# V without a shifted copy, five tiles for transposed probabilities, and PV of unit i-4 ordered behind the scores of unit i

## The chip, the cores and the metric

The kernel runs on one core of a Trainium2 chip. TensorE multiplies matrices, VectorE (DVE), ScalarE (ACT) and GpSimd (POOL) work on elements, and SyncE (SP) issues most transfers from a queue of its own; 16 DMA engines carry them. The engines run beside each other and wait for each other through semaphores; each takes its own instructions strictly in order. The metric is the device time of the whole program in microseconds.

## The reference, cut to what matters

```python
q_rot, k_rot = (rotate(q), rotate(k))          # (4, 8, 576, 64), rotary
scores = scale * np.matmul(q_rot, k_rot.transpose(0, 1, 3, 2))
attn = np.exp(scores - scores.max(-1)) / (sum + 1e-09)
x = np.matmul(attn, v)                         # to (2304, 512)
h = np.maximum(np.maximum(x @ w1, x @ w2), x @ w3)
x = h @ w_out                                  # (2304, 512)
# then each token goes to the expert with the largest logit of x @ w_gate:
out[mask] = gate * (np.maximum(xe @ w1[e], 0.0) @ w2[e])
```

All inputs are float32. The kernel multiplies in float16 pairs: a number is split into a high and a low half, and a product is the sum of high by high, high by low and low by high.

## The kernel before

The program has three parts: attention over 4 batches, a dense layer (the three products, their maximum, `w_out`) whose work is mixed into attention, and the routed layer, which starts after attention at about 606 us.

Attention is cut into 36 units a batch, 144 in all: four query blocks of 128 by eight heads, and four units for the 64 queries that are left. One unit goes through this chain:

- S(i): TensorE multiplies one query block with all 576 keys into a score bank (lines 636, 637 in batch 0, 643 to 646 and 656 later). There are two banks.
- VectorE scales the scores and takes the minimum (659); ScalarE takes the exponential into `p32` and its float16 high half (661, 663).
- VectorE makes the low half (668), 576 columns. `p16` then holds 576 high and 576 low columns side by side.
- SP issues one DMA that transposes the 1152 columns in nine blocks of 128 into a tile `pt` (671). There are three `pt` tiles.
- PV(i): TensorE multiplies the blocks with V in 14 matmuls (695, 696, 698, 699).

576 is four and a half blocks of 128. So the fifth block holds the last 64 high columns and the first 64 low columns, and all later low blocks lie 64 positions off. The kernel therefore keeps a second copy of V's high half, shifted by 64 positions across the partitions, in the same tile (`v2`); two DMAs for each half batch write it (606, 607), and two ScalarE instructions fill its ends (608, 609).

Each batch needs preparation: `prep_qk` loads, rotates, splits and transposes queries and keys of four heads at a time (three transposing DMAs of 18 blocks, lines 485, 486, 490), `prep_v` loads and splits V. Three buffers for transposed keys rotate, so the second half of a batch can only be transposed once the first half of the batch before is through.

A scheduler places the instructions of each engine in a fixed order: each has a priority (`self.at(...)`, in units of attention) and is placed once it believes its inputs to be ready. PV is called `LAG` = 3 units behind S, but its place on TensorE is the scheduler's. Dense-layer matmuls (799 to 801, 847 to 849) carry later priorities and fill in between; here they are called other work.

Of the kernel before, what the change touches and what calls it, by code (L numbers as in the profile page):

```python
# [10 lines left out]
F16 = mybir.dt.float16  # L11
BF16 = mybir.dt.bfloat16
# [10 lines left out]
P = 128  # L23
# [47 lines left out]
class K:  # L71
# [490 lines left out]
    def prep_v(self, b):  # L562
# [4 lines left out]
        def load():  # L567
            if b == 0:
                both = self.att.tile([P, 6, DM], F32, tag="kq0", name="vraw0", bufs=1).rearrange("p f c -> p (f c)")
            for hf in range(2):  # L570
                st["v", hf] = vp.tile([P, 56, D], F16, tag=f"v{hf}", name=f"v{hf}", bufs=1)
# [11 lines left out]
        def stats():  # L583
            sums = self.small.tile([P, 2], F32, name="v_sums")
            for hf in range(2):
                st["v2", hf] = st["v", hf][:, 32:52].rearrange("p (h r) d -> p h r d", h=4)
                nc.scalar.activation(st["v2", hf].rearrange("p a b d -> p (a b d)").bitcast(BF16),
                                     st[hf].rearrange("p a b -> p (a b)"), AF.Square, accum_out=sums[:, hf:hf + 1])
# [8 lines left out]
        def conv(hf):  # L597
            def go():
                s, x = st["s"], st[hf]
                vt, v2 = st["v", hf], st["v2", hf]  # L600
# [4 lines left out]
                vh4 = vh.rearrange("p (h r) d -> p h r d", r=4)  # L605
# [6 lines left out]
                self.V[b, hf] = (vh4, vl.rearrange("p (h r) d -> p h r d", r=4), v2, vt[:, 52:56])  # L612
                self.V[b, "inv"] = st["inv"]
            return go
# [3 lines left out]
    def attention(self, b):  # L618
# [5 lines left out]
        def s_part(i):  # L624
# [5 lines left out]
            if b == 0:  # L630
# [6 lines left out]
                nc.tensor.matmul(ps[:, 1, :64], lhsT=q, rhs=kt[pr, j, 512:S], start=True, stop=True)  # L637
# [605 lines left out]
LAG = 3  # L1243
# [43 lines left out]
```

## Time and profile before

| | us |
|---|---|
| median of 3 runs | 932.07 |
| lowest and highest | 930.55, 932.56 |
| profiled execution | 929.0 |
| its span | 927.2 |
| TensorE busy | 782.3 |
| VectorE busy | 670.2 |
| ScalarE busy | 574.5 |
| GpSimd busy | 249.5 |

The span is the time from the first to the last instruction. TensorE's busy time is modelled and too long, since matmuls overlap; the spacing of their starts in the timeline tells more. A wait is the idle time of an engine before an instruction, put down to what ended it. The granted clock of TensorE is a share of 2.4 GHz; it takes two levels, 1.2 and 2.4 GHz.

### The profile page before, as it was taken

What the parts mean: (1) busy time and instruction counts of PE and PEld (TensorE: products, weight loads), DVE (VectorE), ACT (ScalarE), POOL (GpSimd) and SP (SyncE); (2) the same over time, 40 slices, a digit from 0 to 9 for tenths busy, and PEclk for the clock granted to TensorE, in tenths of its full rate; (3) what the DMA queues carried; (4) which work ended last, traced back from release to release, by engine and by line L of the source; (5) the groups of instructions that cost most, each with busy time, mean ns of one, the idle gap of its engine ahead of it and who ended that gap; (6) DMA issues with size and microseconds to landing.
All of it is one profiled execution on the core that took longest, in us unless ns stands there. A gap on an engine that the chain in (4) does not pass through costs nothing.

```text
span 927.2 us, 18852 instructions
## 1 busy us (share of the span) xinstructions
PE 782.3 (84%) x7304; PEld 641.5 (69%) x7304; DVE 670.2 (72%) x1338; ACT 574.5 (62%) x1001; POOL 249.5 (27%) x245
## 2 busy tenths in 40 slices
PE   2568899889766887879898898995899999998995
PEld 1345677677644666668677677785798889997994
DVE  6988988967796776687765687542848787765771
ACT  3677877745674765565763576521834797774772
POOL 8330003234231042131112100003312744423320
PEclk9995558999987999899989999998899999998999
DMA  8699777994999988979985799713210211133110
GB/s 250 154 218 220 194 141 118 202 176 104 157 165 136 164 140 152 143 129 150 125 132 85 106 144 128 123 39 121 107 31 30 69 47 46 44 117 137 43 36 20
DMA packets 270646, 112.24 MB, mean 121 GB/s; under 512 B 246319, under 2 KB 262847, under 8 KB 270032
## 3 DMA queue, kind: packets, MB, share of 16 engines
q1 hardware_dynamic: 260992, 81.40, 52.5%
q0 software_dynamic: 9552, 29.51, 9.9%
q8 instruction: 61, 1.00, 0.5%
q14 instruction: 41, 0.34, 0.1%
HBM read 74.97 MB, written 9.80 MB: 91 GB/s over the span
## 4 chain that ended last, share of the span: by engine, by line
PE 36%; DMA 15%; issue 4%; DVE 4%; ACT 2%; POOL 2%; SPq 0%; POOLq 0%; ACTq 0%; DVEq 0%
DMA pt<-p 7%; DMA out<-o,di 5%; PE mm L800 4%; PE mm L799 4%; PE mm L801 4%; PE pa L1201 3%; PE pa L1200 3%; PE pa L1202 3%; PE pb L1172 3%; PE pb L1170 3%; PE pb L1171 3%; PE mm L847 1%; PE mm L849 1%; DMA kq<-kls 1%; PE mm L848 1%
## 5 line engine op out<-in xcount | busy, mean ns | idle before, releaser
L799 PE MATMUL mm<-xT,w 128*128 128x256 f16 (+1 forms) x792 | 195.7, 262 | 3.1 <-DVE hm L815 2.6
L800 PE MATMUL mm<-xT,w 128*128 128x256 f16 (+1 forms) x792 | 195.7, 262 | 0.0
L801 PE MATMUL mm<-xT,w 128*128 128x256 f16 (+1 forms) x792 | 195.0, 261 | 0.0
L661 ACT ACTIVATE p<-s,bi 128x576 f32<-128x576 f32 x144 | 105.6, 734 | 82.1 <-DVE s L659 58.7
L668 DVE SCALAR_TENSOR_TENSOR p<-p,p 128x576 f16<-128x576 f32 x144 | 121.5, 846 | 26.8 <-ACT p L663 26.5
L695 PE MATMUL o<-v,pt 128*128 128x64 f16 (+1 forms) x576 | 63.0, 208 | 68.9 <-DMA pt<-p 64.8
L659 DVE TENSOR_SCALAR_CACHE_REDUCE s<-s,qk_sc 128x576 f32<-128x576 f32 x108 | 87.7, 820 | 35.2 <-PE s L646 27.7
L695 PEld LDWEIGHTS <-pt 128*128 128x128 f16 x576 | 47.7, 106 | 84.0 <-DMA pt<-p 76.7
L1109 ACT CAST h<-r 128x512 fp32r<-128x512 f32 x80 | 93.7, 1209 | 18.2 <-DMA r<-moe_w,widx 13.7
L663 ACT ACTIVATE p<-p 128x576 f16<-128x576 f32 x144 | 96.7, 679 | 6.0 <-DMA pt<-p 4.0
L1110 DVE TENSOR_TENSOR l<-r,h 128x512 fp32r<-128x512 f32 x80 | 90.1, 1165 | 5.1 <-ACT h L1109 4.6
L799 PEld LDWEIGHTS <-w 128*128 128x128 f16 x792 | 80.9, 102 | 13.3 <-DVE hm L815 2.0
L800 PEld LDWEIGHTS <-w 128*128 128x128 f16 x792 | 80.2, 101 | 11.1 <-issue 2.7
L801 PEld LDWEIGHTS <-w 128*128 128x128 f16 x792 | 80.7, 102 | 8.8 <-issue 0.7
L1200 PE MATMUL pa<-xh,h 128*128 128x256 f32 x288 | 81.5, 286 | 0.8 <-ACT xh L1131 0.8
L1201 PE MATMUL pa<-xl,h 128*128 128x256 f32 x288 | 81.6, 284 | 0.2 <-DVE xl L1132 0.2
L1202 PE MATMUL pa<-xh,l 128*128 128x256 f32 x288 | 81.6, 284 | 0.0
L847 PE MATMUL mm<-oh,h 128*128 128x256 f16 (+1 forms) x216 | 61.8, 288 | 4.8 <-DVE hm L815 3.4
L1172 PE MATMUL pb<-h,hl 128*128 128x512 f32 x152 | 61.6, 408 | 3.1 <-DVE hl L1204 3.0
L696 PE MATMUL o<-v,pt 128*128 128x64 f16 (+1 forms) x576 | 62.7, 207 | 1.1 <-DVE v L604 1.1
L1170 PE MATMUL pb<-h,hh 128*128 128x512 f32 x152 | 61.6, 408 | 0.9 <-ACT hh L1203 0.9
L927 POOL DMA_INDIRECT islot<-rows,pi x18 | 19.2, 1069 | 159.1 <-DVE pi L917 93.3
(303 smaller groups left out, 2092.4 us busy)
## 6 DMA issues: line engine op xcount, KB each, us to landing
wr<-moe_w POOLq DMA_DIRECT2D x10, 768.0 KB, 5.4
yscr<-y SPq DMA_DIRECT2D x18, 257.0 KB, 3.4
rk<-k SPq DMA_DIRECT2D x8, 512.0 KB, 5.3
vraw<-v SPq DMA_DIRECT2D x8, 512.0 KB, 5.0
rq<-q SPq DMA_DIRECT2D x7, 512.0 KB, 5.5
wr<-moe_w_out POOLq DMA_DIRECT2D x4, 768.0 KB, 6.6
pt<-p SPq DMA_TRANSPOSE x144, 3.9
v<-v SPq DMA_DIRECT2D x16, 128.0 KB, 5.3
```

The source lines that it names most:

```text
L661: nc.scalar.activation(p32, sf, AF.Exp, bias=bi, scale=-1.0, accum_out=st["sum", c][:, h:h + 1])
L663: nc.scalar.activation(p16[:, 0], p32, AF.Copy, scale=32768.0)
L668: nc.vector.scalar_tensor_tensor(out=p16[:, 1], in0=p32, scalar=32768.0, in1=p16[:, 0], op0=ALU.mult, op1=ALU.subtract)
L695: nc.tensor.matmul(out, lhsT=pt[:, blk], rhs=sel(vh, blk), start=blk == 0, stop=False)
L799: nc.tensor.matmul(pv[:, i], lhsT=wh, rhs=xT[:, k, :n], start=k == 0, stop=False)
L800: nc.tensor.matmul(pv[:, i], lhsT=wh, rhs=xT[:, 4 + k, :n], start=False, stop=False)
L801: nc.tensor.matmul(pv[:, i], lhsT=wl, rhs=xT[:, k, :n], start=False, stop=k == 3)
L1109: nc.scalar.copy(T["h1"][:, :, j], r[:, :, j])
L1110: nc.vector.tensor_tensor(out=T["l1"][:, :, j], in0=r[:, :, j], in1=T["h1"][:, :, j].bitcast(F32), op=ALU.subtract)
L1200: nc.tensor.matmul(ps[:, i], lhsT=h1[:, k, j + i], rhs=xh[:, k], start=k == 0, stop=False)
L1201: nc.tensor.matmul(ps[:, i], lhsT=h1[:, k, j + i], rhs=xl[:, k], start=False, stop=False)
L1202: nc.tensor.matmul(ps[:, i], lhsT=l1[:, k, j + i], rhs=xh[:, k], start=False, stop=k == 3)
```

## The change

The low half is put down in another order: its last 64 columns first, then its first 512. The fifth block then holds the last 64 high and the last 64 low columns, and the other low blocks lie on V's own blocks. V's tail of 64 keys is written on both halves of the partitions, as it already was loaded, and its low half is zero on the upper ones. So the shifted copy, its two DMAs and its end pieces go; V shrinks from 56 to 40 rows. The low half is now made by two VectorE instructions. PV still takes 14 matmuls. `LAG` becomes 4, there are five `pt` tiles, and every PV is ordered on TensorE behind the last score matmul of the unit that is called in the same step; this is an order in the queue, with no semaphore.

```diff
 def conv(hf):
-                vh, vl, vlt = vt[:, 0:16], vt[:, 16:32], vt[0:64, 52:56]
-                nc.gpsimd.memset(vt[64:128, 52:56], 0.0)
-                nc.scalar.activation(vh, x[:, 0:16], AF.Copy, scale=s)
-                nc.vector.scalar_tensor_tensor(out=vl, in0=x[:, 0:16], scalar=s, in1=vh, op0=ALU.mult, op1=ALU.subtract)
-                nc.sync.dma_start(v2[0:64, :, 1:5], vh4[64:128])
-                nc.sync.dma_start(v2[64:128, :, 0:4], vh4[0:64])
-                nc.scalar.activation(v2[0:64, :, 0], x[0:64, 16:20], AF.Copy, scale=s[0:64])
-                nc.scalar.activation(v2[64:128, :, 4], x[64:128, 16:20], AF.Copy, scale=s[64:128])
-                nc.vector.scalar_tensor_tensor(out=vlt, in0=x[0:64, 16:20], scalar=s[0:64], in1=v2[0:64, :, 0],
-                                               op0=ALU.mult, op1=ALU.subtract)
+                nc.scalar.activation(vt[:, 0:20], x, AF.Copy, scale=s)
+                nc.vector.scalar_tensor_tensor(out=vt[:, 20:40], in0=x, scalar=s, in1=vt[:, 0:20], op0=ALU.mult, op1=ALU.subtract)
+                nc.gpsimd.memset(vt[64:128, 36:40], 0.0)
 def lo_part(i):
-            nc.vector.scalar_tensor_tensor(out=p16[:, 1], in0=p32, scalar=32768.0, in1=p16[:, 0],
-                                           op0=ALU.mult, op1=ALU.subtract)
+            for o, i0, n in ((S, 512, 64), (S + 64, 0, 512)):
+                nc.vector.scalar_tensor_tensor(out=p16[:, o:o + n], in0=p32[:, i0:i0 + n], scalar=32768.0,
+                                               in1=p16[:, i0:i0 + n], op0=ALU.mult, op1=ALU.subtract)
 def pv_part(i):
-            for blk in range(4):
-                nc.tensor.matmul(out, lhsT=pt[:, blk], rhs=sel(vh, blk), start=blk == 0, stop=False)
-                nc.tensor.matmul(out, lhsT=pt[:, blk], rhs=sel(vl, blk), start=False, stop=False)
-            for blk in range(5):
-                nc.tensor.matmul(out, lhsT=pt[:, 4 + blk], rhs=sel(v2, blk), start=False, stop=False)
-            nc.tensor.matmul(out, lhsT=pt[:, 4], rhs=last(), start=False, stop=True)
+            for blk in range(5):
+                for a in range(2):
+                    nc.tensor.matmul(out, lhsT=pt[:, blk], rhs=sel(a, blk), start=blk + a == 0, stop=False)
+            for blk in range(4):
+                nc.tensor.matmul(out, lhsT=pt[:, 5 + blk], rhs=sel(0, blk), start=False, stop=blk == 3)
...
-                    with self.at(u + i - LAG):
+                    with self.at(u + i - LAG), self.tc.issue_after(self.scored):
                         pv_part(i - LAG)
...
-LAG = 3
+LAG = 4
...
-P16, PT = 4, 3
+P16, PT = 4, 5
```

Three places show what this does to the orders. The first is TensorE in batch 3, at unit 115. Before, with `pt_7238` the transposed probabilities of unit 115 and `s_7363` the scores of unit 118:

```order
L699 LDWEIGHTS pt_7238
L699 MATMUL o_6971<-v1_5448,pt_7238 128x64
L643 LDWEIGHTS kq_4940
L643 MATMUL s_7363<-kq_4940 128x512
L644 LDWEIGHTS kq_4940
L644 MATMUL s_7363<-kq_4940 128x64
```

After, with `pt_7300` the probabilities of unit 115 and `s_7455` the scores of unit 119:

```order
L635 LDWEIGHTS kq_4975
L635 MATMUL s_7455<-kq_4975 128x512
L636 LDWEIGHTS kq_4975
L636 MATMUL s_7455<-kq_4975 128x64
L687 LDWEIGHTS pt_7300
L687 MATMUL o_7084<-v1_5489,pt_7300 128x64
```

PV(115) stood ahead of S(118) and now stands behind S(119).

The second is VectorE at the low half of unit 58 (`p16_3611` before, `p16_3595` after). Before:

```order
L917 CAST pi_3022<-pos_3023 128x2
L668 SCALAR_TENSOR_TENSOR p16_3611<-p32_3609,p16_3611 128x576
L110 TENSOR_SCALAR sc_va_3256<-sc_vb_3257 128x1
L659 TENSOR_SCALAR s_3724,bi_3729<-s_3724,qk_sc_826 128x576
L724 TENSOR_SCALAR r_3424<-sums_3292 128x8
```

After:

```order
L660 SCALAR_TENSOR_TENSOR p16_3523<-p32_3521,p16_3523 128x64
L660 SCALAR_TENSOR_TENSOR p16_3523<-p32_3521,p16_3523 128x512
L660 SCALAR_TENSOR_TENSOR p16_3595<-p32_3593,p16_3595 128x64
L660 SCALAR_TENSOR_TENSOR p16_3595<-p32_3593,p16_3595 128x512
L714 TENSOR_SCALAR r_3472<-sums_3309 128x8
```

One instruction became a short and a long one, back to back; unit 57's pair stands just ahead of unit 58's.

The third is SP's queue near the end of batch 0, at the transposition of unit 30 (`pt_2223` before, `pt_2220` after). Before:

```order
L392 DMA rq_1569<-q 64x2x64
L606 DMA v0_1241<-v0_1241 64x4x256
L607 DMA v0_1241<-v0_1241 64x4x256
L606 DMA v1_1246<-v1_1246 64x4x256
L607 DMA v1_1246<-v1_1246 64x4x256
L671 DMA_TRANSPOSE pt_2223<-p16_2194 128x9x128
```

After:

```order
L392 DMA rq_1581<-q 64x2x64
L490 DMA_TRANSPOSE kq_853<-qs_826 128x18x128
L663 DMA_TRANSPOSE pt_2187<-p16_2148 128x9x128
L663 DMA_TRANSPOSE pt_2220<-p16_2183 128x9x128
L663 DMA_TRANSPOSE pt_2248<-p16_2216 128x9x128
```

The four copies of V are gone from between the loads and the transposition, and the transposition of queries now stands behind the loads.

## Rows read from the trace of the kernel before

**Rows 1.** Stretches: us, then busy us (count) of PE, PEld, DVE, ACT, POOL, clock.

```profile
60.00:180.00 120.00, 103.89 (x889) 77.75 (x886) 108.26 (x226) 94.66 (x179) 22.81 (x24) 0.67 0.85 177
180.00:340.00 160.00, 128.64 (x1487) 100.45 (x1488) 117.90 (x263) 97.86 (x196) 41.23 (x38) 0.91 0.96 155
340.00:480.00 140.00, 115.89 (x1398) 93.44 (x1396) 103.28 (x242) 87.78 (x179) 32.22 (x30) 0.93 0.85 134
480.00:606.00 126.00, 112.77 (x1347) 91.89 (x1346) 86.74 (x204) 71.02 (x154) 11.36 (x14) 0.96 0.79 118
606.00:928.00 322.00, 293.41 (x2078) 260.59 (x2076) 204.86 (x337) 189.64 (x231) 106.80 (x90) 0.96 0.19 63
```

**Rows 2.** Timeline of TensorE: starts of PV, dense-layer and score matmuls.

```profile
286.22 0.19 PE L695 MATMUL o<-v,pt 128*128 128x64 f16 x1
286.25 0.19 PE L696 MATMUL o<-v,pt 128*128 128x64 f16 x1
...
509.75 0.27 PE L800 MATMUL mm<-xT,w 128*128 128x256 f16 x1
509.86 0.27 PE L801 MATMUL mm<-xT,w 128*128 128x256 f16 x1
...
510.51 0.38 PE L643 MATMUL s<-kq 128*128 128x512 f16 x1
510.73 0.19 PE L644 MATMUL s<-kq 128*128 128x64 f16 x1
```

**Rows 3.** TensorE's waits from 180 to 606 us: total us, times, longest.

```profile
PE o L695 <- DMA pt<-p: 56.5, 40, 6.0
PE s L643 <- ACT p L661: 5.6, 6, 2.2
```

**Rows 4.** Transpositions, slot scatters: landing times; then two of SP's waits.

```profile
DMA to landing us min/median/max: 3.2/3.9/9.3
DMA to landing us min/median/max: 6.4/8.1/12.0
SPq L671 <- DVE p L668: 132.9, 65, 9.1
SPq L671 <- PE o L699: 27.3, 26, 2.9
```

**Rows 5.** Timeline: start us, us, engine; a wait and its end in brackets.

```profile
269.56 0.20 PE L695 MATMUL o<-v,pt 128*128 128x64 f16 x1 [2.04 <-DMA pt<-p]
282.42 3.04 SPq L671 DMA_TRANSPOSE pt<-p  x2
283.00 1.28 POOL L927 DMA_INDIRECT islot<-rows,pi  x1 [2.81 <-DVE pi L917]
293.20 0.24 PE L695 MATMUL o<-v,pt 128*128 128x64 f16 x1 [6.00 <-DMA pt<-p]
```

**Rows 6.** VectorE: four instructions of the timeline, then two groups (busy, mean ns).

```profile
98.10 0.15 DVE L113 TENSOR_SCALAR sc_ws<-sc_wa 128x1 int32<-128x1 int32 x1
98.16 0.14 DVE L320 TENSOR_SCALAR winv<-sc_wa 128x1 f32<-128x1 f32 x1
...
102.02 0.70 DVE L668 SCALAR_TENSOR_TENSOR p<-p,p 128x576 f16<-128x576 f32 x1
102.64 0.95 DVE L309 SCALAR_TENSOR_TENSOR w<-wv,w 128x768 int32<-128x768 int32 x1
...
L332 DVE SCALAR_TENSOR_TENSOR w<-w,wscl 128x768 f16<-128x768 f32 x12 | 12.1, 1011 | 0.7 <-ACT w L331 0.7
L604 DVE SCALAR_TENSOR_TENSOR v<-vraw,sc_vs,v 128x1024 f16<-128x1024 f32 x8 | 10.2, 1279 | 2.0 <-ACT v L603 1.9
```

**Rows 7.** V's preparation: two groups, and TensorE's wait for the copy.

```profile
L608 ACT ACTIVATE v<-vraw,sc_vs 64x256 f16<-64x256 f32 x8 | 4.0, 495 | 0.0
L610 DVE SCALAR_TENSOR_TENSOR v<-vraw,sc_vs,v 64x256 f16<-64x256 f32 x8 | 4.8, 598 | 0.0
PE o L698 <- DMA v<-v: 1.9, 1, 1.9
```

**Rows 8.** Timeline of SP: first copy of V and the next transposition.

```profile
173.60 0.62 SPq L606 DMA_DIRECT2D v<-v  x1
...
177.15 1.36 SPq L671 DMA_TRANSPOSE pt<-p  x1
```

**Rows 9.** Timeline: batch 1's second query transposition, then the scores that used it.

```profile
213.78 2.73 SPq L490 DMA_TRANSPOSE kq<-qs  x1
...
219.32 0.39 PE L643 MATMUL s<-kq 128*128 128x512 f16 x1
```

More of the change, by code (lines that the diff above doesn't have):

```diff
@@ L570, in load @@
             for hf in range(2):
-                st["v", hf] = vp.tile([P, 56, D], F16, tag=f"v{hf}", name=f"v{hf}", bufs=1)
+                st["v", hf] = vp.tile([P, 40, D], F16, tag=f"v{hf}", name=f"v{hf}", bufs=1)
                 if b == 0:
@@ L636, in s_part @@
                 nc.tensor.matmul(ps[:, 0], lhsT=q, rhs=kt[pr, j, 0:512], start=True, stop=True)
-                nc.tensor.matmul(ps[:, 1, :64], lhsT=q, rhs=kt[pr, j, 512:S], start=True, stop=True)
+                ins = nc.tensor.matmul(ps[:, 1, :64], lhsT=q, rhs=kt[pr, j, 512:S], start=True, stop=True)
             elif c < 4:
@@ L645, in s_part @@
                 nc.tensor.matmul(ps[:, 0], lhsT=qt[:, qb], rhs=kl[:, hh * 4:hh * 4 + 4], start=False, stop=True)
-                nc.tensor.matmul(ps[:, 1, :64], lhsT=qt[:, qb], rhs=kl[:, 16 + j, 64 * o:64 * o + 64], start=False, stop=True)
+                ins = nc.tensor.matmul(ps[:, 1, :64], lhsT=qt[:, qb], rhs=kl[:, 16 + j, 64 * o:64 * o + 64], start=False, stop=True)
             else:
@@ L655, in s_part @@
                             out, rhs = (ps[pr, 1, :64], kk[:, 16 + j, pr]) if tail else (ps[pr, 0], kk[:, hh * 4:hh * 4 + 4])
-                            nc.tensor.matmul(out, lhsT=qt[:, 16 + j, pr], rhs=rhs, start=first, stop=not first)
+                            ins = nc.tensor.matmul(out, lhsT=qt[:, 16 + j, pr], rhs=rhs, start=first, stop=not first)
+            self.scored = ins.ins
             sf = ps.rearrange("p a b -> p (a b)")[:, 0:S]
@@ L661, in s_part @@
             nc.scalar.activation(p32, sf, AF.Exp, bias=bi, scale=-1.0, accum_out=st["sum", c][:, h:h + 1])
-            p16 = self.pw.tile([P, 2, S], F16, tag="p16", name="p16", bufs=P16)
-            nc.scalar.activation(p16[:, 0], p32, AF.Copy, scale=32768.0)
+            p16 = self.pw.tile([P, 2 * S], F16, tag="p16", name="p16", bufs=P16)
+            nc.scalar.activation(p16[:, :S], p32, AF.Copy, scale=32768.0)
             st[i] = (p32, p16)
@@ L683, in pv_part @@
                 hf, hh = divmod(h, 4)
-                vh, vl, v2, vlt = self.V[b, hf]
+                vt = self.V[b, hf].rearrange("p (a x) d -> p a x d", a=2)
                 out = o_ps[:, 64 * h:64 * h + 64]
-                sel = lambda t, blk: t[:, hh, blk]
-                last = lambda: vlt[:, hh]
+                sel = lambda a, blk: vt[:, a, 4 * hh + blk if blk < 4 else 16 + hh]
             else:
                 hf, j = divmod(h, 2)
-                vh, vl, v2, vlt = self.V[b, hf]
+                vt = self.V[b, hf].rearrange("p (a x) d -> p a x d", a=2)
                 out = o_ps[:, 128 * h:128 * h + 128]
-                sel = lambda t, blk: t[:, j::2, blk]
-                last = lambda: vlt[:, j::2]
-            for blk in range(4):
-                nc.tensor.matmul(out, lhsT=pt[:, blk], rhs=sel(vh, blk), start=blk == 0, stop=False)
-                nc.tensor.matmul(out, lhsT=pt[:, blk], rhs=sel(vl, blk), start=False, stop=False)
-            for blk in range(5):
-                nc.tensor.matmul(out, lhsT=pt[:, 4 + blk], rhs=sel(v2, blk), start=False, stop=False)
-            nc.tensor.matmul(out, lhsT=pt[:, 4], rhs=last(), start=False, stop=True)
+                sel = lambda a, blk: (vt[:, a, 0:16].rearrange("p (h r) d -> p h r d", r=4)[:, j::2, blk] if blk < 4
+                                      else vt[:, a, 16 + j:20:2])
+            for blk in range(5):
+                for a in range(2):
+                    nc.tensor.matmul(out, lhsT=pt[:, blk], rhs=sel(a, blk), start=blk + a == 0, stop=False)
+            for blk in range(4):
+                nc.tensor.matmul(out, lhsT=pt[:, 5 + blk], rhs=sel(0, blk), start=False, stop=blk == 3)
             if h == (7 if c < 4 else 3):
```

11 lines of the change are left out of this document (4 added, 7 removed).

## The prediction

> **What bounds the kernel now.** I read the stretches first, then who waited for whom, then single waits in the timeline. The routed stage behind 606 us takes 322 us and holds no line of the change [rows 1]; everything is decided in the attention stage before it. There no engine is full: from 180 to 606 us TensorE is busy 357 of 426 us, VectorE 308, ScalarE 257 [rows 1]. From 60 to 180 us VectorE is busy 108 of 120 us, so there it is close to the bound [rows 1]. TensorE's ends are modelled, so its real load is lower still: 256 columns follow each other every 0.11 us, a 512-column score matmul takes 0.22 us of its stream, a PV matmul 0.03 us [rows 2]. The stage is therefore set by latency, by engines that wait for each other in a fixed order. The largest such wait on TensorE is PV's first matmul for the transposed probabilities: 56.5 us in 40 waits from 180 to 606 us, against 5.6 us for all score matmuls that wait for a score bank [rows 3]. The reader should see why it arises: a transposition lands 3.9 us after its issue at the median but 9.3 us at worst, and a GpSimd scatter of slots takes 8.1 us to land [rows 4]. In the longest wait, 6.00 us at 293.20, the transposition was issued between 282.42 and 285.46, a scatter stood in the DMA engines from 283.00 on, and TensorE had nothing else in its order [rows 5].
>
> **What the change does, step by step.** S(i) is the score product of unit i, PV(i) its product with V. The profiled execution took 929.0 us, 3 us under the median 932.07; I sum differences and put them on the median.
>
> **Term 1, the order on TensorE.** In the order before, PV(i) stands on average behind S(i+3.23): 83 of 144 units behind S(i+3) or an earlier one, 52 behind S(i+4), 9 behind S(i+5). After it is 3.89, with 127 at exactly four. Before, 88 PVs stand directly behind other work, that is where the scheduler believed the transposition had landed; after, 101 stand directly behind S(i+4), so they were believed ready earlier and have slack. Adding up the TensorE work between the end of S(i) and PV(i) in both orders with the spacings of [rows 2] gives 9.8 us before and 11.7 us after as the mean of batches 1 to 3, and 6.6 and 6.7 us in batch 0. So batches 1 to 3 gain 1.9 us of cover per unit and batch 0 gains none. Taking 1.9 us off each of the waits of [rows 3]: eleven are longer, from 2.04 to 6.00 us [rows 5], 35.1 us in all, and keep 35.1 - 11 x 1.9 = 14.2 us; the others vanish. 56.5 - 14 is a gain of 42 us. The other bound is nothing: done unit by unit, with each unit's own two distances, the new waits of units whose distance shrinks eat the gain, and in the trace the 52 units at distance four wait nearly as long (0.50 us a unit, all waits of batch 0 too) as the 57 at distance three (0.63 us a unit). That bookkeeping keeps every delay on the unit it hit, though the scatters and the long transpositions will meet other units. I take **-18 us**, a little under half of 42. Behind a PV that no longer waits the next late thing is a score bank, priced at 5.6 us now [rows 3]. No wait on a semaphore is added; PV(i-4) now queues behind S(i) and S(i)'s own wait for a bank, and those who wait for PV are a transposition five units on and, after every eighth unit, the division on VectorE.
>
> **Five tiles** instead of three: with three, a transposition may not start before PV(i-3) is done. SP waited for PV's last matmul 27.3 us in 26 pieces, none over 2.9 us, but 132.9 us for low parts [rows 4]: the tile is seldom what is late. It buys little alone, but with four units in flight three tiles would stop the queue. No separate term.
>
> **Term 2, the low part in two pieces.** 144 VectorE instructions of 576 columns become 144 of 512 and 144 of 64. The columns stay; 144 fixed costs are added. Back to back, two one-column instructions start 0.06 us apart, and a 576-column low part is followed after 0.62 us, hardly more than its columns [rows 6]: 144 x 0.06 = 8.6 us of VectorE. The upper bound is the fixed part of a duration: 768 columns take 1.011 us and 1024 take 1.279 us, so 1.047 ns a column and 0.207 us fixed [rows 6], 144 x 0.207 = 29.8 us. Nearest is the back-to-back spacing, since both pieces read the same ready data. The 36 units of batch 0 run where VectorE is 90% busy and land in whole, 2.2 us; of the other 6.5 us I let under half land, as VectorE idles 28% there [rows 1]: **+5 us**, bounds 0 and +30. Should the pieces run without overlap, the cover is gone and the upper bound holds.
>
> Here a rule speaks against the change. The Trainium skill, "VectorE: DVE Perf Modes", section on the TRN2 errata, says that each SBUF-sourced instruction pays a fixed latency, about 150 cycles as measured there, and advises tiles of at least 512 elements. By it the price would be an estimated 144 x 0.156 = 22.5 us instead of 8.6; no run here shows a 64-column piece yet.
>
> **Term 3, V without the copy.** Eight times it removes two SP issues and transfers, two ScalarE instructions of 0.50 us and one VectorE instruction of 0.60 us [rows 7], and widens the remaining two by 256 columns (0.27 us on VectorE by its slope, taken for ScalarE too). ScalarE gets 6 us back and VectorE 2.6 us; both have idle time, so I count none of ScalarE's. On the path are PV's wait for the copy, 1.9 us once [rows 7], and the queue: at 173.60 four copies were issued ahead of a transposition that then started at 177.15, 3.55 us [rows 8]. **-4 us**, bounds -8 and 0.
>
> **Term 4, the clock.** The granted clock was 0.91, 0.93 and 0.96 in the three stretches from 180 us on [rows 1], which is some 59 us at 1.2 instead of 2.4 GHz, in pieces that follow waits. Fewer waits, fewer pieces: **-2 us**, bounds -10 and 0.
>
> Sum: -18 + 5 - 4 - 2 = -19, so 929.0 - 19 = 910 for an execution like the profiled one, and 932.07 - 19 = **913 us** as the median.
>
> **The rivals.** *The waits stay* (chance 0.20): the long landings hit whichever unit is in flight, so terms 1 and 4 are nothing: 932 + 5 - 4 = 933. For it: the 0.50 against 0.63 us above. Against: 101 PVs that were believed ready early.
>
> *VectorE takes the place of the wait, slower* (0.13): the short piece costs the whole 0.207 us and, because the transposition waits for the second piece and the next score's minimum stands behind it, all of it reaches the path. 932 - 18 + 30 - 4 - 2 = 938. It decides from 24/144 = 0.17 us landing per unit on. For it: 90% busy before 180 us; against: 28% idle after. By the skill's 22.5 us, same page, the sum would be 930.6, no change.
>
> *All cover works* (0.13): 42 us go, and with them 5 us of clock: 932 - 42 + 5 - 4 - 5 = 886.
>
> *The queue moves a key transposition back* (0.08): S of the second half of each new batch waits for that half's keys, which are transposed late, the query part at 213.78 the first time [rows 9]. On SP, batch 2's second half has its low key part after the transposition of unit 72 instead of straight behind its high part. That is some 14 us later by the trace's rate, covered by 41 more matmuls of other work (41 x 0.11 = 4.5 us): about +10 us, 923.
>
> **How the numbers follow.** Forecast 0.46 at 913, give or take 11. A measurement here tells 0.2%, 1.9 us, from no change. Faster: the forecast, all cover, most of the moved transposition (0.07) and a little of the waits that stay (0.03), 0.69. Same: the middle of the waits that stay and rims of two others, 0.09. Slower: 0.10 of the waits that stay, 0.12 of VectorE's, 0.22. The range runs from 888 to 938: below lies most of the all-cover case, above half of VectorE's case and the rim of the second.
>
> **What will show it.** Term 1: PV's wait for transposed probabilities from 180 us on falls from 56.5 to about 35 us. Term 2: the 64-column piece's start to the next start, 0.06 or 0.2 us. Term 3: first PV complete well before 50 us, and no SP issue between the query part and the next transposition near 173 us. Term 4: granted clock above 0.93 from 180 us on. I am wrong if PV waits as long as before with the same longest landings, if S waits for its bank far beyond 5.6 us, or if the end of the attention stage does not come before 606 us.

## The result and the profile after

The changed kernel takes 935.48 us in the median (926.43 to 940.31), the kernel before 929.06 us on the same chip, ratio 1.0063 [1.0034, 1.0091]: slower by 0.6%, where 2% faster was forecast. The profiled executions stand closer together, 930.15 us (span 928.4) against 929.0, since executions of one kernel scatter by about 1%. So the 6 us rest on the medians; from the profiles I read only what grew and what shrank.

The stretches of the kernel after, columns as in [rows 1]:

```profile
60.00:180.00 120.00, 108.66 (x788) 77.34 (x787) 104.15 (x251) 92.17 (x175) 19.91 (x24) 0.74 0.81 175
180.00:340.00 160.00, 134.85 (x1597) 107.46 (x1597) 122.46 (x311) 100.69 (x198) 36.05 (x34) 0.91 0.91 148
340.00:480.00 140.00, 115.46 (x1407) 93.19 (x1406) 108.69 (x269) 84.50 (x172) 33.70 (x34) 0.91 0.86 131
480.00:606.00 126.00, 111.11 (x1341) 90.94 (x1342) 88.12 (x240) 70.14 (x151) 11.14 (x14) 0.97 0.78 115
606.00:928.00 322.00, 289.85 (x2061) 257.63 (x2058) 202.98 (x335) 188.83 (x230) 105.66 (x90) 0.96 0.19 63
```

TensorE did 101 matmuls fewer than before from 60 to 180 us and 110 more from 180 to 340. From there on the counts differ by 9 and 6: what was gained by 340 us only made up for the early loss. The last PV ends at 601.6 us (603.7 before), but the first gather of the routed stage starts at 637.5 us, as before (637.3).

TensorE's waits in the kernel after, 180 to 606 us, to be held against [rows 3]:

```profile
PE o L687 <- DMA pt<-p: 38.6, 24, 6.6
PE s L633 <- ACT p L652: 9.9, 5, 6.9
PE mm L837 <- DVE hm L805: 8.4, 5, 3.5
```

PV's wait fell from 56.5 to 38.6 us, 17.9 us, almost the forecast amount. Next to it the waits for a score bank and for the dense layer's maximum grew, and TensorE's idle time in this stretch (426 us less its busy time) fell by 4.1 us only, from 68.7 to 64.6 us. The chain that ended last is known for the kernel before from 334 us on, where it breaks off, and for the kernel after from its start. So the two can be compared from 340 to 606 us. Shares of this stretch by line, first the kernel before, then the kernel after:

```profile
by line: DMA pt<-p 25.2%; PE mm L800 8.5%; PE mm L799 8.4%; PE mm L801 8.4%; issue 5.9%; DMA kq<-kls 5.0%; PE o L695 2.9%; PE s L643 2.8%; PE s L645 2.7%; PE mm L849 2.7%; PE o L698 2.6%; POOL t L405 2.5%; PE mm L847 2.4%; PE mm L848 2.4%; 
by line: DMA pt<-p 16.1%; issue 13.2%; DVE p L660 8.4%; DVE s L650 5.6%; DMA kq<-kls 4.3%; ACT p L652 4.2%; DMA vraw<-v 3.5%; ACT p L654 3.2%; PE mm L790 2.9%; PE mm L791 2.9%; PE mm L789 2.9%; PE o L687 2.6%; DMA kq<-qs 2.2%; DMA rq<-q 2.1
```

The transpositions (`DMA pt<-p`) hold less of the chain than before, 42.9 instead of 67.1 us. More of it goes through VectorE, above all through the low part (line 660): 22.4 us, where the chain's pieces of line 668 sum to 4.0 us before.

The low part in the kernel after, busy us and mean ns behind the bar:

```profile
L660 DVE SCALAR_TENSOR_TENSOR p<-p,p 128x64 f16<-128x64 f32 (+1 forms) x288 | 132.4, 503 | 28.3 <-ACT p L654 28.2
```

It was 121.5 us for 144 instructions before: 10.9 us more for the 144 added ones, 0.076 us each.

### The profile page after: what moved, and what is told of

Read it like the earlier page. It is cut to its first block, busy times and chain, and to the rows that moved or that the text cites. A ratio compares the mean times of both kernels' runs of the same rounds, so it can differ in the third digit from the quotient of the medians.

```text
span 928.4 us, 19058 instructions
## 1 busy us (share of the span) xinstructions
PE 789.5 (85%) x7304; PEld 644.2 (69%) x7304; DVE 676.1 (73%) x1474; ACT 567.8 (61%) x985; POOL 240.3 (26%) x245
## 4 chain that ended last, share of the span: by engine, by line
PE 29%; DMA 23%; DVE 19%; issue 17%; ACT 8%; POOL 3%; SPq 1%; POOLq 0%; ACTq 0%; DVEq 0%
DMA pt<-p 8%; DVE p L660 5%; DVE s L650 3%; PE pb L1162 3%; PE pa L1191 3%; PE pa L1192 3%; PE pa L1190 3%; PE pb L1160 3%; PE pb L1161 3%; ACT p L652 2%; DMA kq<-kls 2%; DMA kq<-khs 2%; DMA wr<-moe_w 2%; ACT p L654 2%; PE mm L789 2%
## 5 line engine op out<-in xcount | busy, mean ns | idle before, releaser
L660 DVE SCALAR_TENSOR_TENSOR p<-p,p 128x64 f16<-128x64 f32 (+1 forms) x288 | 132.4, 503 | 28.3 <-ACT p L654 28.2
L687 PE MATMUL o<-v,pt 128*128 128x64 f16 (+1 forms) x1440 | 79.3, 207 | 39.1 <-DMA pt<-p 38.6
L687 PEld LDWEIGHTS <-pt 128*128 128x128 f16 x1440 | 64.0, 105 | 59.9 <-DMA pt<-p 48.5
L654 ACT ACTIVATE p<-p 128x576 f16<-128x576 f32 x144 | 96.5, 678 | 4.7 <-DMA pt<-p 2.8
L626 PE MATMUL s<-kq 64*128 64x512 f32 (+1 forms) x72 | 64.9, 1027 | 15.0 <-ACT p L652 14.9
L837 PE MATMUL mm<-oh,h 128*128 128x256 f16 (+1 forms) x216 | 63.0, 294 | 13.3 <-DVE hm L805 11.8
L839 PE MATMUL mm<-oh,h 128*128 128x256 f16 (+1 forms) x216 | 62.2, 295 | 1.4 <-DVE h L819 1.4
L838 PE MATMUL mm<-ol,h 128*128 128x256 f16 (+1 forms) x216 | 63.2, 295 | 0.0
```

The costliest lines, as they stand in the source:

```text
L654: nc.scalar.activation(p16[:, :S], p32, AF.Copy, scale=32768.0)
L660: nc.vector.scalar_tensor_tensor(out=p16[:, o:o + n], in0=p32[:, i0:i0 + n], scalar=32768.0, in1=p16[:, i0:i0 + n], op0=ALU.mult, op1=ALU. ...
L687: nc.tensor.matmul(out, lhsT=pt[:, blk], rhs=sel(a, blk), start=blk + a == 0, stop=False)
```

## The experiments

Every ratio is to the kernel before on the same chip, with a 95% interval; 0.001 is 0.93 us. Each edit changes what the scheduler believes, so places far from the edit are ordered anew.

**Were late keys the lid?** VectorE's minimum of the first scores of each batch's second half started as late as before (unit 40 at 220.0 us before and 219.2 after, unit 76 at 356.9 and 358.0, unit 112 at 505.6 and 504.8). This suggests theory K: the keys of the second half are late whatever PV does. Theory D: the second VectorE piece ate the gain. Theory O: the new order costs elsewhere what it saves. In two kernels, made from before and from after, the second half's scores of batches 1 to 3 read the keys and queries of the first half.

```diff
-                kh, kl, qt, sc = self.KQ[b, hf]
+                kh, kl, qt, sc = self.KQ[b, 0]
```

> The kernel before, but from batch 1 on the scores of the second four heads read the keys and queries of the first four, so no score waits for the second half's preparation; that preparation is still done in full. Theory K (the late keys of each batch's second half set the pace of batches 1 to 3, so PV's waits lie in time that is waited for anyway): 10 to 30 us faster than the kernel before, with the first score of the second half no longer at 219, 356 and 505 us. Theory D (VectorE's extra piece ate the gain) and theory O (PV behind the scores costs as much as it saves) say nothing of this kernel by itself: by them no more than 5 us.

> The changed kernel with the same edit: second-half scores read the first half's keys and queries. Theory K: with the lid off, the change pays; 5 to 20 us faster than the run before_free. Theory D: 4 to 8 us slower than before_free, as after is slower than before. Theory O: the same as D, with waits of scores for a bank above 15 us.

Measured: 1.0125 [1.0085, 1.0165] and 0.9993 [0.9961, 1.0025]. In the first the minima of units 40, 76 and 112 started at 196.9, 346.2 and 490.5 us, but the last PV ended at 614.0 instead of 603.7. So theory K's first forecast failed: without the late keys the kernel before even lost 1.2%. Its second forecast came out, against theory D: between these two kernels the change is worth 14.9 us (950.72 and 935.85), and PV's waits from 60 to 606 us are 31 us shorter:

```profile
PE o L695 <- DMA pt<-p: 79.5, 39, 7.6
PE o L687 <- DMA pt<-p: 48.1, 20, 10.7
```

Where no score waits for late keys, shorter waits thus came with a shorter time, in one pair of kernels. The edit also keeps the first half's key buffer in use to the end of its batch; no run shows what that costs.

Two others prepare queries ahead of keys:

```diff
-        seq = [load, stats, self.rope_of(st, "k", b), split_k, tr_k, self.rope_of(st, "q", b), split_q, tr_q]
+        seq = [load, stats, self.rope_of(st, "q", b), split_q, self.rope_of(st, "k", b), split_k, tr_k, tr_q]
```

> The kernel before with one line reordered: in each half batch's preparation the queries are rotated and split ahead of the keys, so that after a key buffer comes free only three transpositions are left, and no rotation of queries on GpSimd. Theory K: the first scores of the second halves start 10 to 20 us earlier than 219, 356 and 505 us, and the kernel is 8 to 25 us faster than before. Theories D and O: within 5 us of before.

> The changed kernel with the same reordered preparation, queries ahead of keys. Theory K: faster than before_q_first by 3 to 15 us, since PV's shorter waits are no longer waited for at the batch's start. Theory D: slower than before_q_first by 4 to 8 us. Theory O: slower by as much, with scores waiting for banks longer than in before_q_first.

Measured: 1.0038 [1.0007, 1.0068] and 1.0201 [1.0157, 1.0244]. This edit did not do what it was for: the three minima started at 216.4, 365.0 and 506.6 us in the first kernel and at 231.7, 370.8 and 517.8 in the second, so this pair does not test theory K. Between the two the change costs 15.5 us. Theory K stays open for the kernel after. And the same change brings 14.9 us or costs 15.5 us, depending on what else stands in the orders: no price below is more than a price in its own surroundings.

**The change in parts.** First the kernel after with the low part in one instruction, then V's new layout with the two pieces alone (`LAG` 3, three tiles, no order), then the kernel after without the order, then one in which batch 0's PVs come two at a time. The last tests theory P: in batch 0 a score product uses 64 rows of TensorE, and two neighbours in its queue run side by side. The timeline of TensorE shows it in before, where four matmul instructions of two such products start at 103.89 and take 2.09 us together; in after the two of a single product take 2.07 (the granted clock was 0.50, the lower level, in both places):

```profile
103.89 2.09 PE L636 MATMUL s<-kq 64*128 64x512 f32 x4
```

```profile
101.77 2.07 PE L626 MATMUL s<-kq 64*128 64x512 f32 x2
```

In the written order nine pairs of batch 0's units are neighbours before and one after, since PV stands between them; batch 0's scores take 72.3 us of TensorE instead of 59.8, counted from each start to the next.

```diff
-            for o, i0, n in ((S, 512, 64), (S + 64, 0, 512)):
-                nc.vector.scalar_tensor_tensor(out=p16[:, o:o + n], in0=p32[:, i0:i0 + n], scalar=32768.0, ...)
+            nc.vector.scalar_tensor_tensor(out=p16[:, S:], in0=p32, scalar=32768.0, in1=p16[:, :S], ...)
```

> The kernel after, with the low part of the probabilities in one VectorE instruction of 576 columns again (its two blocks then stand in the wrong order for the product with V; the amount of work of every other instruction is the same). Theory D (the second piece ate the gain): VectorE loses about 10 us of busy time and the kernel gets 5 us faster than the kernel after, ratio to before about 1.001. Theory P (in batch 0 the score products of neighbouring units ran side by side on TensorE, and the order behind the scores parts them; 12.5 us of TensorE in all): the pieces don't matter, ratio 1.006, batch 0's score products stay near 72 us of TensorE where they were 60 before. Theory O (the order costs elsewhere what it saves in PV's waits): 1.004 to 1.006.

```diff
-                    with self.at(u + i - LAG), self.tc.issue_after(self.scored):
+                    with self.at(u + i - LAG):
-LAG = 4
+LAG = 3
-P16, PT = 4, 5
+P16, PT = 4, 3
```

> The kernel after without the order on TensorE: three units of distance and three tiles as before, so that only V without its copy and the two-piece low part are left of the change. The prediction's terms 2 and 3 give -4 + 5 = +1 us, ratio 1.001. Theory D: the pieces cost more than 5 us, ratio 1.005 or more. Theory P: the neighbours in batch 0 are parted less (the written order has three neighbouring pairs, 9 before, 1 after), so batch 0's score products take some 68 us against 60 and 72, and the ratio is between 1.000 and 1.004. Theory O: the time is that of before or under it, since what costs is the order; PV waits some 56 us from 180 to 606 us.

```diff
-                    with self.at(u + i - LAG), self.tc.issue_after(self.scored):
+                    with self.at(u + i - LAG):
```

> The kernel after without the order of PV behind the scores, all else kept: four units of distance, five tiles. Theory O: PV's waits rise again towards 50 us but the other waits fall (scores for a bank from 25 to 15 us), the time falls by 3 to 6 us below the kernel after, ratio 0.999 to 1.003. Theory P: three neighbouring pairs instead of one in batch 0, a gain of 2 us at most, ratio 1.004. Theory D: no change against the kernel after, 1.006.

```diff
-                if i - LAG >= 0:
+                for k in ((i - LAG,) if b else (i - LAG - 1, i - LAG) if i % 2 else ()):
+                    if k >= 0:
```

> The kernel after, with batch 0's PVs issued two at a time behind the second unit of a pair, so that the two score products of a pair can stand next to each other on TensorE (six neighbouring pairs in the written order; 9 before, 1 after). Batches 1 to 3 keep the order behind the scores. Theory P: batch 0's score products fall from 72 to about 64 us of TensorE, dense work starts earlier, and the time falls by 5 to 8 us below the kernel after, ratio 0.998 to 1.001. Theories D and O: the score products may fall as said but the time stays that of the kernel after, 1.006, since TensorE is not what the early stage waits for.

Measured: 1.0001 [0.9973, 1.0028], 1.0067 [1.0030, 1.0104], 1.0078 [1.0044, 1.0113] and 1.0041 [1.0009, 1.0072]. One piece gives back 5.8 us, theory D's number. Without the order the time is not lower, so theory O in its simple form falls. In the pairs kernel batch 0's scores took 67.4 us, and 2 us of time were gained, within the intervals: theory P explains little at most.

Then the pieces alone on the kernel before, and V's layout alone with one piece:

```diff
-            nc.vector.scalar_tensor_tensor(out=p16[:, 1], in0=p32, scalar=32768.0, in1=p16[:, 0], ...)
+            for o, n in ((0, 64), (64, 512)):
+                nc.vector.scalar_tensor_tensor(out=p16[:, 1, o:o + n], in0=p32[:, o:o + n], scalar=32768.0, ...)
```

> The kernel before, with one edit: its low part in two pieces, 64 and 512 columns (same data, same place). Theory D (the 144 added VectorE instructions cost the time, mostly through a later start of the dense layer in the early stage where VectorE is full): as much as between the kernel after and its one-piece version, +5 to +6 us, ratio 1.006; the first dense matmul comes at 114 us or later instead of 110.7, and some 75 instead of 104 of the first kind are done by 180 us. Rival, the pieces hurt only together with the new order or with V's new layout: 1.000 to 1.002.

The second is the kernel of V's layout alone with the one-instruction low part shown above.

> V without its copy as the only change: three units of distance, three tiles, no order behind the scores, and the low part in one instruction (its two blocks in the wrong order for the product with V, the work otherwise the same). The prediction's term 3: -4 us, ratio 0.996. Theory D: the copy's work and its SP place were hidden, ratio 0.999 to 1.001; then the order adds nothing either, since the one-piece kernel with the order measured 1.0001. If it comes out under 0.996, the order costs what V's part gives.

Measured: 1.0076 [1.0041, 1.0111] and 1.0063 [1.0029, 1.0097]. The pieces alone cost 7 us. The place that I had expected did not hold: 100 first dense matmuls were done by 180 us, not 75 (104 before, 72 after). Nor does that count tell the time: V's layout alone has 106 with one piece and 72 with two, at the same time. V's layout alone costs 5.9 us where I had seen a gain or nothing. The table of ratios:

| | low part in one | in two |
|---|---|---|
| V as before, order as before | 1 | 1.0076 |
| V's new layout, order as before | 1.0063 | 1.0067 |
| V's new layout, new order, five tiles | 1.0001 | 1.0063 |

Each ratio is known to some 0.35%. The parts do not add up: with one piece the order brings 5.8 us, with two nothing clear; and the second piece costs 7.1 us, 0.4 us and 5.8 us in the three rows.

**What PV's waits are worth.** PV takes a constant tile, so no transposition holds it; all other work runs. There are four `pt` tiles instead of five.

```diff
-            pt = st.pop(i)
+            st.pop(i)
+            pt = self.ptc
-P16, PT = 4, 5
+P16, PT = 4, 4
```

> The kernel after, with PV's product taking a constant tile instead of the transposed probabilities, so that PV never waits for a transposition; transpositions and all else still run (outputs are not the reference's). This is the price of PV's waits, 38.6 us of TensorE idle time in the kernel after. By the prediction's rate (18 us of time for 18 us of wait): 25 to 38 us faster than the kernel after, ratio 0.966 to 0.980. Theory W (TensorE's idle time is not what sets the stage; the waits move to the score banks and to dense matmuls that wait for their inputs): at most 8 us faster, ratio 0.998 to 1.006, with the waits for a bank and for the dense layer's inputs grown by 15 us or more.

> The one-piece kernel (1.0001, with 46.2 us of PV waits before the routed stage) with PV's product taking a constant tile, so that no PV waits (outputs are not the reference's, all other work runs). Theory VT (the second VectorE piece took the place of PV's waits): without the piece the waits pay, 8 us or more, ratio 0.991 or less. Theory W (PV's waits cost nothing, other waits replace them): ratio 0.997 to 1.003, and TensorE's idle time before the routed stage stays between 95 and 120 us (105.0 in the one-piece kernel).

Measured: 1.0061 [1.0017, 1.0105] with two pieces (1.0063 with the waits) and 0.9997 [0.9967, 1.0026] with one (1.0001 with the waits). **Taking all of PV's waits away gives nothing** that these intervals could tell from zero (5 us with two pieces, 4 us with one). What grew in their place is in the rows of TensorE's and of ScalarE's waits, 60 to 606 us. Two pieces (the 14.8 us stand before a dense matmul that reads no transposed probabilities, so what ended them is not certain):

```profile
PE s L636 <- ACT p L655: 28.9, 18, 8.1
PE mm L793 <- DMA pt<-p: 14.8, 1, 14.8
...
ACT p L657 <- DMA pt<-p: 26.4, 12, 5.6
ACT qs L436 <- DMA rq<-q: 19.0, 2, 9.7
```

One piece:

```profile
PE s L636 <- ACT p L655: 48.1, 21, 15.6
...
ACT p L657 <- DMA pt<-p: 27.0, 8, 6.5
```

With PV's waits in place ScalarE's high part waited for transpositions 2.8 us (two pieces) and 13.6 us (one piece), and scores of batches 1 to 3 waited for a bank 9.9 and 10.3 us. There are four `p16` tiles: ScalarE's high part of unit i cannot be written before the transposition of unit i-4 has read its tile. So a late transposition that no longer stops TensorE can stop ScalarE, behind it wait the exponentials, and behind these the score banks. All of ScalarE's waits for a DMA in this stretch sum to 49 us with two pieces and 61 with one, and to 89 and 93 in these two kernels. TensorE's idle time, 546 us less its busy time, does not fall: 75.9 and 76.4 us with the waits, 83.8 and 81.2 without. The stretches of the four, columns as in [rows 1], then the busy share of the DMA engines and GB/s: two pieces with and without the waits, one piece with and without.

```profile
60.00:606.00 546.00, 470.09 (x5131) 368.93 (x5131) 423.42 (x1069) 347.50 (x693) 100.80 (x105) 0.89 0.85 142
60.00:606.00 546.00, 462.19 (x5049) 366.62 (x5047) 417.64 (x1056) 344.68 (x686) 101.81 (x105) 0.85 0.94 143
60.00:606.00 546.00, 469.57 (x5121) 370.09 (x5121) 413.61 (x928) 344.51 (x691) 111.65 (x104) 0.89 0.86 143
60.00:606.00 546.00, 464.79 (x5060) 367.48 (x5059) 407.89 (x916) 341.03 (x685) 107.04 (x104) 0.85 0.92 141
```

They show that the edit took away more than the waits. The DMA engines moved as much as before but were busy 0.94 and 0.92 of the time instead of 0.85 and 0.86, and ScalarE's waits for loads and other transfers grew too, by 16 and 18 us. And the minimum of unit 76, the first of batch 2's second half, started at 371.7 and 370.0 us instead of 358.0 and 360.7. So two rivals stay beside the ring of `p16` tiles: later landings that the edit itself brought, and the late keys of theory K. A kernel with the constant tile and without late keys was not run.

The longest wait for a score bank, 15.59 us, in the timeline of the one-piece kernel, whose profiled execution was the slowest of twelve (start us, us, engine; the wait in brackets):

```profile
440.31 5.51 SPq L391 DMA_DIRECT2D rq<-q  x1
...
459.65 1.16 ACT L436 ACTIVATE qs<-rq 128x1152 bf16<-128x1152 f32 x1 [10.79 <-DMA rq<-q]
...
460.81 0.72 ACT L655 ACTIVATE p<-s,bi 128x576 f32<-128x576 f32 x1
...
461.67 0.58 PE L636 MATMUL s<-kq 128*128 128x512 f16 x1 [15.59 <-ACT p L655]
```

A load of the next half's queries was late, ScalarE's sum of squares stood in its queue ahead of an exponential, and TensorE waited for that exponential's bank. The kernel after has the like at 370 us, with V's load:

```profile
358.34 0.61 SPq L581 DMA_DIRECT2D vraw<-v  x1
...
367.69 1.27 ACT L586 ACTIVATE v<-vraw 128x1280 bf16<-128x1280 f32 x1 [7.89 <-DMA vraw<-v]
...
369.53 0.72 ACT L652 ACTIVATE p<-s,bi 128x576 f32<-128x576 f32 x1
...
370.39 0.59 PE L633 MATMUL s<-kq 128*128 128x512 f16 x1 [6.90 <-ACT p L652]
```

**The pieces, moved and doubled.** In one kernel the split goes to ScalarE: the low part stands first, in one VectorE instruction, and ScalarE writes the last 64 high columns twice.

```diff
-            nc.scalar.activation(p16[:, :S], p32, AF.Copy, scale=32768.0)
+            nc.scalar.activation(p16[:, S + 64:], p32, AF.Copy, scale=32768.0)
+            nc.scalar.activation(p16[:, S:S + 64], p32[:, 512:S], AF.Copy, scale=32768.0)
...
+            nc.vector.scalar_tensor_tensor(out=p16[:, :S], in0=p32, scalar=32768.0, in1=p16[:, S + 64:], ...)
-P16, PT = 4, 5
+P16, PT = 4, 4
```

> The kernel after, right in all outputs, with the split moved from VectorE to ScalarE: the low part stands first in the tile and is one VectorE instruction, and ScalarE writes the high part's last 64 columns a second time (144 small ScalarE instructions); four tiles for transposed probabilities, since five no longer fit. Theory D: the VectorE price is gone, the ScalarE price is hidden (ScalarE idles 40% from 180 us on), ratio 0.999 to 1.002. Rival, ScalarE's pieces delay the exponentials in the early stage (ScalarE is busy 41 of 60 us from 60 us on) as VectorE's pieces did: 1.005 or more.

```diff
-            for o, i0, n in ((S, 512, 64), (S + 64, 0, 512)):
+            for o, i0, n in ((S, 512, 64), (S + 64, 0, 256), (S + 320, 256, 256)):
```

> The kernel after with the low part in three pieces (64, 256 and 256 columns): 144 VectorE instructions more, some 11 us of VectorE at the 0.076 us that a piece added. If the second piece's price was its work: +5 to +7 us again, ratio 1.011 to 1.014. If it was the chance of another order: ratio anywhere from 1.000 to 1.008, no step of that size.

Measured: 0.9989 [0.9949, 1.0030] and 1.0178 [1.0116, 1.0241]. On ScalarE the added pieces, 35.0 us of its time, cost nothing clear against the one-piece kernel (1.0001). On VectorE a third piece costs another 1.15%, 10.7 us, for 19.1 us more busy time:

```profile
L660 DVE SCALAR_TENSOR_TENSOR p<-p,p 128x256 f16<-128x256 f32 (+1 forms) x432 | 151.5, 405 | 7.6 <-ACT p L654 6.7 <-issue 0.3
```

So under the new order a little over half of what is added to VectorE comes through: 5.8 of 10.0 us between one and two pieces, then 10.7 of 19.1. The rate is not general: on the kernel before it is 7.1 of 23.7 us, under V's layout with the order before 0.4 of 12.8.

**Which engine sets the pace.** Work was taken off each engine in the kernel after: VectorE's 512-column piece, 512 columns of ScalarE's high part, one of three products of the dense layer.

```diff
-            for o, i0, n in ((S, 512, 64), (S + 64, 0, 512)):
+            for o, i0, n in ((S, 512, 64),):
```

> The kernel after without the 512-column piece of the low part (the tiles that are transposed hold a constant there; outputs differ from the reference in that part): some 107 us of VectorE busy time go, 0.74 us per unit, everything else runs. Theory V (VectorE's chain of minimum, low part and dense-layer work sets the pace of the attention stage): 25 us or more faster than the kernel after, ratio 0.98 or less. Theory T (TensorE's total work sets the end, waits only move on it): at most 8 us, ratio 0.998 or more. Theory L (no engine's work, but the order written in advance): under 5 us, 1.001 to 1.006.

```diff
-            nc.scalar.activation(p16[:, :S], p32, AF.Copy, scale=32768.0)
+            nc.scalar.activation(p16[:, 512:S], p32[:, 512:S], AF.Copy, scale=32768.0)
```

> The kernel after with ScalarE's copy into the high part cut from 576 to 64 columns (constants elsewhere; the low part's product differs from the reference accordingly): some 60 to 70 us of ScalarE go, 144 copies of 0.68 us become copies of 0.2 to 0.25 us. Theory V: ScalarE's copy stands ahead of the low part, so 10 to 20 us, ratio 0.985 to 0.996. Theories T and L: under 5 us, 1.001 to 1.006.

```diff
                         nc.tensor.matmul(pv[:, i], lhsT=wh, rhs=xT[:, 4 + k, :n], ...)
-                        nc.tensor.matmul(pv[:, i], lhsT=wl, rhs=xT[:, k, :n], start=False, stop=k == 3)
```

> The kernel after with two instead of three products in the dense layer's first matmuls (the weights' low part is left out there): 792 matmuls of 256 or 128 columns go from TensorE, some 74 us of its time before the routed stage and 6 behind. Theory T: 50 us or more faster, ratio 0.95 or less. Theory V: the attention stage keeps its pace, and only the dense work that is left at its end, some 35 us, goes, with the 6 us behind: 25 to 40 us faster, ratio 0.965 to 0.98, with the last PV at 595 us or later. Theory L: as V.

Measured: 1.0011 [0.9976, 1.0045], 0.9891 [0.9842, 0.9940] and 0.9726 [0.9675, 0.9778], against 1.0063. The rows of the first two, to be held against 132.4 and 96.5 us in the kernel after:

```profile
L664 DVE SCALAR_TENSOR_TENSOR p<-p,p 128x64 f16<-128x64 f32 x144 | 44.4, 311 | 40.2 <-ACT p L658 39.1
```

```profile
L658 ACT ACTIVATE p<-p 128x64 f16<-128x64 f32 x144 | 35.7, 252 | 15.6 <-DMA pt<-p 13.2
```

88 us off VectorE bring 5 us, no more than one piece did; 61 us off ScalarE bring 16 us; some 80 us off TensorE (792 matmuls, an estimate by the spacing of their starts) bring 31. The last kernel's stretch from 60 to 606 us:

```profile
60.00:606.00 546.00, 431.13 (x4534) 327.80 (x4533) 423.49 (x1069) 348.94 (x698) 105.68 (x105) 0.82 0.86 142
```

TensorE idles 115 us here and its granted clock is lower (0.82; after 0.89): part of the relief turned into waits and into time at the lower of the two clocks, 1.2 instead of 2.4 GHz. In its profiled execution, the slowest of six, the last PV ended at 604.0 us (601.6 after): attention kept its pace, as theories V and L had it. No theory fits whole: V's forecasts held in the second and third kernel, L's in the first and third, T's in the first. VectorE hurts when loaded and hardly helps when relieved, and no engine gives back half of what is taken off it.

Last, the kernel with 64 low columns, without PV's waits:

> The kernel with only 64 columns of the low part left (1.0011, 107 us of VectorE gone, 44.2 us of PV waits), with PV's product taking a constant tile as well. Theory VT: VectorE has room now, so the waits pay at least half of their length, ratio 0.978 or less. Theory W: ratio 0.995 to 1.004. If it falls between (0.980 to 0.993), the waits are worth something only where VectorE is far from full.

Measured: 0.9913 [0.9884, 0.9943], 1.0% under the same kernel with its waits. With 88 us off VectorE, 44 us of PV's waits are worth 9 us, a fifth; with VectorE as it is, nothing. This is between theory VT, that the second piece took the waits' place, and theory W, that they cost nothing. As an account of the whole loss VT falls, since without the piece the waits bring nothing either. ScalarE waits for transpositions here too (7.3 us with PV's waits in place), and the DMA engines' busy share rose from 0.86 to 0.94:

```profile
ACT p L660 <- DMA pt<-p: 33.1, 9, 9.0
```

## Why the prediction was wrong, point by point

**What bounds the kernel.** "Set by latency, by engines that wait for each other in a fixed order" fits the runs: no engine gave back half of what was taken off it. What failed is the next step: the largest wait on TensorE was taken as the price of the stage. What was late was the transposition's landing, and PV was the first to meet it. The median landing is 3.9 us in both kernels, the longest 9.3 us before and 11.7 after; the change did not bring the landings forward.

**Term 1, forecast -18 us.** The waits fell as forecast, 56.5 to 38.6 us. That each us of wait is a us of time is the step that failed: with all the waits gone the time was 1.0061 against 1.0063, and 0.9997 against 1.0001 with one piece. TensorE idled as long, and ScalarE waited some 40 and 32 us more for transfers. Why the time stayed is open between the ring of `p16` tiles, later landings and late keys; and in the pair without late keys, 31 us less of these waits did come with 14.9 us less time. The prediction named the next late thing, "a score bank, priced at 5.6 us", and took the price from a trace in which PV still met the lateness first. Once it did not, that price rose to 9.9 us, and to 28.9 and 48.1 us where PV never waited.

**Five tiles.** No run separates them from the order. That there was no term for them fits the untied kernel, which has the five tiles and calls PV four units behind and is no faster (1.0078) than the one with three of both (1.0067).

**Term 2, forecast +5 us, bounds 0 and +30.** Right in two of three pairs: 5.8 us between one and two pieces under the new order, 7.1 us alone, but 0.4 us under V's layout with the order before. The size of a piece came near: in a median unit the two pieces take 0.82 us from first start to last end, one took 0.75, so 0.07 us where 0.06 was taken. By sums of busy time it is 0.07 to 0.165 us in the three pairs. The Trainium skill's 150 cycles ("VectorE: DVE Perf Modes", section on the TRN2 errata), an estimated 0.156 us a piece, are twice this 0.07 us; its direction, that small tiles cost on VectorE, held in three of the four steps (the third piece, 10.7 us, is the fourth). The cover named (28% idle VectorE) hid about half of the work under the new order, as assumed, and more elsewhere. But work on VectorE does not pay at the same rate when it is taken off: eight times as much gave 5 us.

**Term 3, forecast -4 us, bounds -8 and 0.** Its signs were there: the first PV was complete at 48.5 us (50.2 before), and behind the query transposition at 167.62 SP goes straight to the next unit's:

```profile
167.62 3.71 SPq L490 DMA_TRANSPOSE kq<-qs  x1
171.50 4.86 SPq L663 DMA_TRANSPOSE pt<-p  x3
```

The time was not: V's layout alone measured +5.9 us, outside the bounds. This is a second step that failed: work and queue places taken away were priced as time won, and the time rose. The profile of that kernel (928.3 us, well under its median of 935.3) shows ScalarE's wait for the query load up from 11.0 to 25.9 us, 16.4 in one piece; whether that is the cause stays open, because one profile cannot carry 6 us here.

**Term 4, forecast -2 us.** The mean granted clock was 0.913 before and 0.921 after; from 180 to 606 us it was 0.93 in both, not above. It did not order the times: of the 20 executions of the kernel after, ten had 0.945 to 0.956 and a median of 935.4 us, nine had 0.881 to 0.899 and 935.8 us; the two shortest spans of all profiled runs, 916.6 and 916.9 us (less ScalarE work, less TensorE work), had 0.893 and 0.875, and the span of 932.5 us of the ScalarE split had 0.955.

**The rivals.** As a ratio the time is that of "VectorE takes the place" (938 to 932.07, 1.0064), in us it lies between this and "the waits stay" (933). The number was met by luck: that rival kept the 18 us of term 1 and priced a piece at 0.2 us in full. Each rival had a part of the mechanism: waits did not stay on TensorE as they were, but TensorE's idle time and others' waits did, and VectorE's added piece came through, at about half its work. The moved key transposition had no part (unit 76 at 356.9 and 358.0 us). The chances went wrong where "the waits stay" got only 0.20: its test was whether the same PVs wait as long, and I asked nowhere whether the wait could move to another engine. The range held the time, by its upper end.

In sum, along one path of the table: V's layout +5.9 us (forecast -4), the order with five tiles -5.8 (forecast -18), the pieces +5.8 (forecast +5), together +5.9, the measured 0.63%. Along the other path, pieces first, they are +7.1, -0.8 and -0.4. So no part has a price of its own, and which of them made the 6 us is not shown. No kernel run here that leaves nothing out beats both by a measurable amount: the ScalarE split, 0.9989, is 7 us faster than the kernel after and level with before.

What stays open: where in the program the pieces' 6 us fall, why V's layout alone costs time, whether PV's waits would pay if no score waited for late keys, and whether the DMA engines, busy 0.87 of the time from 60 to 606 us before and 0.85 after, are what makes the landings late. The last two were not tried.

## What to carry to other kernels

A wait shows who met a late thing first, and not yet what its lateness costs; before pricing it, follow the late buffer to everyone else who needs it (here the four `p16` tiles that ScalarE refills), and ask what would wait there. A cheap way to learn the price is to run the kernel once with a constant in place of the awaited data, and then to look whether the transfers still land as before. Work added to an engine can cost where taking as much away brings little, so a cheap instruction per unit should go to the engine that the runs show to have room, which here was ScalarE. And where every edit orders the program anew, a part of 0.6% should be measured in more than one surrounding before it is called its price.

## What was not expected of the hardware

Two score products that use 64 rows of TensorE each ran side by side when they were neighbours in its queue: four matmul instructions in 2.09 us, two in 2.07. In the kernel after batch 0's scores took 12.5 us more of TensorE, of which the time showed nothing clear. The order behind the scores is only a part of this: V's layout with two pieces, without that order, has 67.1 us, 7.3 more than before.

A VectorE instruction of 64 columns was followed by the next after 0.137 us, of which some 0.067 are its columns by the slope of [rows 6]: the rest, 0.07 us, is far under the 0.207 us that the durations gave as the fixed part.
